# Linear attention and a squared-ReLU MLP on one Trainium2 core: the last queries of the first two batches transposed together

## The chip, the core and the metric

The kernel runs on one core of a Trainium2 chip. TensorE (PE) multiplies matrices and writes to PSUM; VectorE (DVE) and ScalarE (ACT) work element by element; SyncE (SP) issues the loads and stores; GpSimd (POOL) does almost nothing here. The metric is device time in microseconds (us), the median over runs.

## The reference

```
kv  = einsum('bhsd,bhse->bhde', k, v)            # 8 batches, 8 heads, 576 rows, 64 features
out = einsum('bhsd,bhde->bhse', q, kv)
x   = out / sqrt(mean(out * out, -1) + 1e-6) * g_norm
x   = x.transpose(0, 2, 1, 3).reshape(4608, 512)
g   = maximum(x @ w_in, 0) ** 2                  # w_in 512 x 2048
out = g @ w_out                                  # w_out 2048 x 512
```

The weights arrive as float64 and are converted to float32 on the chip.

## The kernel before

**Attention.** For each batch b and pair of heads p, `transposed_query(b, p)` brings the queries into the layout with features on the partitions, and `key_value(b, p)` forms the 64x64 products of keys and values. A batch has 576 rows: four tiles of 128, and 64 rows left over. The left-over rows of two batches make one more tile of 128; for batches 0 and 1 these are the last queries, `q_rest[0]`, loaded by two DMAs of 64 rows (L156). In batches 0 and 1 queries are transposed on PE (L339) into a PSUM tile `t_ps` and copied out by ACT (L341); with b = 1, each call also transposes two heads of `q_rest` into `tr_ps` (L345) and copies them into `qT_rest` (L348). In later batches DVE transposes. Products of keys and values gather in `kv_ps` (L357), and two ACT copies (L359, L360) take them to `kv_all`. `t_ps`, `kv_ps` and the later `xt_ps` share the tag "at" of a PSUM pool with two buffers, taken by turns. `products_x` (L388) multiplies queries by key-value products into `x_ps`; it reads `qT_rest` for the left-over rows. Then come squares on ACT (L397), sums and inverse roots on DVE (L400 to L411) and the scaled rows `x_n` (L429), which are transposed (L475) for the MLP. In the text, T(b, p) stands for the transposed query and kv(b, p) for the keys-values of that batch and pair.

**Weights.** They are loaded as 32 raw pieces, 16 of each matrix (L198), into a pool of eight buffers; each is converted by two ACT instructions (L210, L213) and four on DVE (L222 to L231). The last pieces of w_out are summed into blocks `wt` and stored to a scratch tensor in DRAM (L281), from which `w_blk` is loaded later (L662, L665).

**MLP.** The 4608 rows are taken in nine strips of 512. The first strip's up-projection runs plainly (L614), into PSUM tags A (two buffers), B and C (one each), which ACT reads with Relu and Square (L621, L622). Its down-projection and all later strips use sums of blocks so that seven products do for eight (L578, L768), with DVE forming the sums (L248, L605); in the first strip's down-projection the sums of the weight blocks (`w_t`) are also stored to DRAM (L698).

**Order.** The schedule is written out by hand: each engine takes its instructions strictly in the order in which the program issues them, and waits where an operand or a buffer is not ready. Attention work is a list `slices`; the loop over the MLP's steps calls `attend(n)` after each step, which issues slices up to index n. During the first strip, one slice of batch 1 follows each step from the sixth last up-projection step on: T, kv, T, kv, and so on. With `n` counting those steps, the eight slices of batch 1 fill n = 1 to 8; then groups of four slices (query, normalized, two of features) follow by threes. Each step also calls `convert` for weights, and starts loads on SP's queue: those of batch 1's pairs, of the left-over keys and values (L148), and of `q_rest` (L156), between steps 5 and 9.

Of the kernel before, what the change touches and what calls it, by code (L numbers as in the profile page):

```python
# [10 lines left out]
FP32 = mybir.dt.float32  # L11
# [9 lines left out]
def kernel(  # L21
# [34 lines left out]
    nc = tc.nc  # L56
    P = 128
# [4 lines left out]
    NP = H // 2  # L62
    FC = d_ff // P
    C = S // P
# [10 lines left out]
    Q_ON_PE = 2  # L75
# [17 lines left out]
    apsum = ctx.enter_context(tc.tile_pool(name="apsum", bufs=2, space=bass.MemoryType.PSUM))  # L93
# [46 lines left out]
    q_rest = {}  # L140
# [3 lines left out]
    def load_rest(b, eng):  # L144
        h = b % 2
        half = slice(REST * h, REST * (h + 1))
        for t, src in ((k_rest[half], k), (v_rest[half, h], v)):
            eng.dma_start(out=t, in_=src[b, :, C * P : S].rearrange("h s d -> s h d"))  # L148

    def load_q_rest(b, eng):  # L150
        h = b % 2
        if h == 0:
            q_rest[b // 2] = rest_pool.tile([P, H, D], FP32, name="q_rest", tag="q_rest")
        src = q[b, :, C * P : S]
        if b < Q_ON_PE:
            eng.dma_start(out=q_rest[b // 2][REST * h : REST * (h + 1)], in_=src.rearrange("h s d -> s h d"))  # L156
            return
        t = squares(q_rest[b // 2])
        for a in range(4):
            hq, f = divmod(a * SQ, D)  # L160
            for kq in range(2):
                eng.dma_start(
                    out=t[ts(a, SQ), 2 * h + kq], in_=src[hq::2, ts(kq, SQ), f : f + SQ].rearrange("p i f -> i p f")
                )
# [4 lines left out]
    def load_next(q_eng=nc.sync):  # L169
        u = next(to_load, None)  # L170
        if u is not None:
            load(*u, q_eng)
# [82 lines left out]
    def sums_in(g):  # L255

        nc.scalar.activation(w_in[:, :, g, 0:4], w_in[:, :, g, 0:4], AF.Copy, scale=g_col)
        a11, a21, a12, a22, s1, s2, s4 = (w_in[:, :, g, b] for b in range(7))
        nc.vector.tensor_tensor(out=s1, in0=a21, in1=a22, op=ALU.add)
        minus(nc.vector, s2, s1, a11)  # L260
        minus(nc.vector, s4, a12, s2)
        minus(nc.vector, a21, a11, a21)
# [24 lines left out]
    def convert(n):  # L287
        while converted[0] < min(n, len(conversions)):
            fn, a = conversions[converted[0]]
            fn(a)  # L290
            converted[0] += 1

    ident = const.tile([P, P], FP32, name="ident")
# [23 lines left out]
    qT, kvd, x_n, xt = {}, {}, {}, {}  # L317
    flat = lambda t: t.rearrange("p h d -> p (h d)")

    def open_rest(b):  # L320
        t = qt_pool.tile([P, NP, P], FP32, name="qT_rest", tag="qT_rest", bufs=1)
        for p in range(NP):
            qT["rest", b // 2, p] = t[:, p]
        return t

    def transposed_query(b, p):
        t = main.pop(("q", b, p))
        if b >= Q_ON_PE:
            qT[b, p] = qt_pool.tile([P, C, P], FP32, name="qT", tag="qT")
            nc.vector.transpose(out=flat(qT[b, p]), in_=flat(t))  # L330
            if b % 2 and p == NP - 1:
                nc.vector.transpose(
                    out=open_rest(b).rearrange("p q (k t) -> p q k t", k=4),
                    in_=squares(q_rest[b // 2]).rearrange("p k q f -> p q k f"),
                )
            return
        ps = apsum.tile([P, C, P], FP32, name="t_ps", tag="at")
        for c in range(C):
            nc.tensor.transpose(ps[:, c, :], flat(t[:, c]), ident)  # L339
        qT[b, p] = qt_pool.tile([P, C, P], FP32, name="qT", tag="qT")  # L340
        nc.scalar.copy(qT[b, p], ps)  # L341
        if b % 2:
            t = q_rest[b // 2][:, 2 * p : 2 * p + 2]
            ps = apsum.tile([P, 2, C * P], FP32, name="tr_ps", tag="x", bufs=1)[:, 0, 0:P]
            nc.tensor.transpose(ps, flat(t), ident)  # L345
            if p == 0:
                open_rest(b)
            nc.scalar.copy(qT["rest", b // 2, p], ps)  # L348

    def key_value(b, p):  # L350
        tk, tv = main.pop(("k", b, p)), main.pop(("v", b, p))
# [157 lines left out]
    slices, ready = [], {}  # L509
# [10 lines left out]
    for b in range(1, B):  # L520
        for p in range(NP):
            slices += [(transposed_query, (b, p)), (key_value, (b, p))]
        first_n = b // 2 * PAIR + (C if b % 2 else 0)
        ns = list(range(first_n, first_n + C + b % 2))
        for i in range(0, len(ns), 2):
            slices += [(query, (ns[i : i + 2],)), (normalized, (ns[i : i + 2],))]
            for n in ns[i : i + 2]:
                slices.append((features if b < X_ON_PE else squares_x, (n,)))
                if n % NT == NT - 1:
                    ready[n // NT] = len(slices)  # L530
    slice_at = [0]

    def attend(n):
        while slice_at[0] < min(n, len(slices)):
            fn, a = slices[slice_at[0]]
            fn(*a)
            slice_at[0] += 1
# [64 lines left out]
    def sums_g(s, g):  # L602
        dest = quarters(s, g)
        s1 = gq[s, 1, g] = sum_pool.tile([P, 2, TH], FP32, name="g_s1", tag="sum")
        nc.vector.tensor_tensor(out=s1, in0=dest[12], in1=dest[22], op=ALU.add)  # L605
        minus(nc.vector, dest[12], dest[11], dest[12])
# [134 lines left out]
    def leaf_sums(s, p):  # L741
        a = gq[s, A_G[p]]
        a11, a12, a21, a22 = (a[:, ts(f, FQ // 2), ts(t, P)] for t in range(2) for f in range(2))
        s1, s2, s3, s4 = (sum_pool.tile([P, FQ // 2, P], FP32, name=f"g_s{i}", tag="sum") for i in range(4))
        leaf[p] = {1: a11, 2: a12, 3: s4, 4: a22, 5: s1, 6: s2, 7: s3}
        nc.vector.tensor_tensor(out=s1, in0=a21, in1=a22, op=ALU.add)
        minus(nc.vector, s2, s1, a11)
        minus(nc.vector, s4, a12, s2)
        minus(nc.vector, s3, a11, a21)
# [85 lines left out]
    for s in range(N_STRIP):  # L835
        attend(ready[s])
        if s == 0:
            steps = [(2, up_first, (g, fh, i)) for g in range(NG) for fh in range(2) for i in range(2)]
        else:
            steps = [(1, up, (s, g, p)) for g in range(NG) for p in ORDER]  # L840
        n_up = len(steps)
        if s < DEEP:

            steps += [(2, down, (s, p, i)) for p in (ORDER if s else (1, 2, 5, 6, 7, 3, 4)) for i in range(2)]
        else:
            steps += [(2, down_deep, (s, k, i)) for k in range(7) for i in range(2)]
        goal = ready.get(s + 1, len(slices))
        total, done = sum(w for w, _, _ in steps), 0
        for i, (w, fn, a) in enumerate(steps):
            if s == 0 and i < n_up:  # L850

                convert(5 + (3 * i + 2) // 4)
                if i in (5, 7, 9):
                    load_next()
                if i == 6:
                    load_q_rest(0, nc.sync)
                    load_rest(1, nc.sync)
                    load_q_rest(1, nc.sync)
            elif s == 0 and i == n_up:
                convert(len(conversions))  # L860
                conv.close()
                sum_pool = ctx.enter_context(tc.tile_pool(name="sum", bufs=8, reuse_waits="tile"))
                stream_pool = ctx.enter_context(tc.tile_pool(name="stream", bufs=4, reuse_waits="tile"))
            if s == 0 and n_up <= i < n_up + NG:
                sums_g(0, i - n_up)
            fn(*a)
            done += w
            if s:
                attend(ready[s] + int((goal - ready[s]) * min(done / (0.42 * total), 1)))
                if s >= DEEP and i == n_up - 3:  # L870
                    leaf_sums(s, 4)
                continue
            if i == n_up + 11:
                load_next()
            if i == n_up + 13:
                load_rest(2, nc.sync)
                load_q_rest(2, nc.sync)
            if i - n_up in (7, 9, 11, 13):
                sums_in((i - n_up - 7) // 2)
            if i == n_up + 11:  # L880
                sums_x(1)
            if i == len(steps) - 1:
                stream(2)

            n = i + 1 - (n_up - 6)
            pairs, m = divmod(max(n - 2 * NP, 0), 3)
            attend(min(ready[0] + min(max(n, 0), 2 * NP) + 4 * pairs + (0, 2, 2)[m], goal))


# [28 lines left out]
```

## Time and profile before

| | |
|---|---|
| median of nine runs | 940.37 us (939.13 to 942.24) |
| the profiled execution's own time | 940.37 us |
| its span | 938.5 us |
| PE busy | 912.4 us, 97% |
| DVE busy | 685.2 us, 73% |
| ACT busy | 226.0 us, 24% |
| the four transposes of `q_rest` (L345) | 0.27 to 0.30 us each, starting between 74.2 and 101.0 us |
| their four copies (L348) | 0.27 us each |
| PE waiting for the load of `q_rest` | 3.9 us, once |
| DMA, mean over the span | 204 GB/s; 282 GB/s between 64 and 72 us |

Matmuls overlap in the pipeline, so the distance between two starts says more of their cost than the duration of one. A wait in the profile is time in which an engine stood, with the event that ended it. A granted clock below 1.00 means that PE's work took longer by that ratio.

### The profile page before, as it was taken

Reading aid. Unit: us, or ns where it says so; the run is one execution under the profiler, and the core shown is the slowest. Engines: PE = TensorE matmul, PEld = TensorE weight load, DVE = VectorE, ACT = ScalarE, POOL = GpSimd, SP = SyncE. Lnnn points to the kernel's source line nnn. Section 1 sums busy time; section 2 is a strip of 40 time slices with the busy share of each in tenths; the row PEclk is TensorE's granted clock in tenths of the full one; section 3 lists DMA queues with packets and bytes.
Section 4 is the critical chain, followed back from the end, with each engine's and each line's share of the span. In section 5 each row is a group of like instructions: output and inputs, shape, how many; then the busy total and the mean of one; then the engine's idle time right before and its main releaser. Section 6 shows DMA issues by size and latency. Waiting matters only on the chain.

```text
span 938.5 us, 17429 instructions
## 1 busy us (share of the span) xinstructions
PE 912.4 (97%) x7048; PEld 807.0 (86%) x7048; DVE 685.2 (73%) x1195; ACT 226.0 (24%) x497; POOL 1.7 (0%) x7
## 2 busy tenths in 40 slices
PE   5898999999999999999999999999999999999998
PEld 4444877889988998899889998899889988998898
DVE  4998887479846995489748974697559854983496
ACT  4796342220023102310222013201220022002200
POOL 0000000000000000000000000000000000000000
PEclk9899999999999999999999999999999999999999
DMA  9799988746964585558564875477516831682075
GB/s 280 260 285 297 310 289 294 202 112 243 303 177 99 211 291 183 128 165 320 190 145 134 297 242 138 98 292 253 173 27 246 290 99 57 235 289 71 0 262 176
DMA packets 165295, 191.46 MB, mean 204 GB/s; under 512 B 84064, under 2 KB 137824, under 8 KB 156640
## 3 DMA queue, kind: packets, MB, share of 16 engines
q1 hardware_dynamic: 164896, 190.23, 63.2%
q8 instruction: 55, 0.90, 0.4%
q14 instruction: 24, 0.20, 0.1%
q10 hardware_dynamic: 320, 0.13, 0.1%
HBM read 159.12 MB, written 31.20 MB: 203 GB/s over the span
## 4 chain that ended last, share of the span: by engine, by line
PE 87%; DVE 6%; DMA 3%; issue 1%; ACT 1%; SPq 1%; DVEq 0%; ACTq 0%
PE ps_A L578 25%; PE ps_B L768 21%; PE ps_A L768 16%; PE ps_B L578 13%; PE ps_C L578 6%; PE kv_ps L357 2%; PE x_ps L388 2%; DVE w_c L228 1%; PE ps_C L614 1%; DMA w_blk<-w_out 1%; DVE w_in L231 1%; PE ps_A L614 1%; DMA q_rest<-in_q_dram 1%; DVE w_c L222 1%; DMA raw<-in_moe_w_in_dram 1%
## 5 line engine op out<-in xcount | busy, mean ns | idle before, releaser
L578 PE MATMUL ps_A<-x_t,w_in 128*128 128x256 f32 x768 | 183.1, 381 | 0.0
L578 PEld LDWEIGHTS ps_A<-x_t,w_in 128*128 128x128 f32 x768 | 144.5, 190 | 20.1
L768 PE MATMUL ps_B<-w_blk,g_s 128*128 128x128 f32 x1024 | 124.8, 275 | 0.0
L768 PEld LDWEIGHTS ps_B<-w_blk,g_s 128*128 128x128 f32 x1024 | 119.5, 192 | 0.0
L768 PE MATMUL ps_B<-w_blk,gt 128*128 128x128 f32 x768 | 96.2, 275 | 0.0
L768 PE MATMUL ps_A<-w_blk,g_s 128*128 128x128 f32 x768 | 93.6, 275 | 0.0
L768 PEld LDWEIGHTS ps_B<-w_blk,gt 128*128 128x128 f32 x768 | 91.5, 192 | 0.4
L768 PEld LDWEIGHTS ps_A<-w_blk,g_s 128*128 128x128 f32 x768 | 89.6, 192 | 0.0
L637 DVE TENSOR_TENSOR gt<-ps_A,snap 128x512 f32<-128x512 f32 x32 | 22.1, 690 | 75.4 <-PE ps_A L578 75.4
L768 PE MATMUL ps_A<-w_blk,gt 128*128 128x128 f32 x576 | 72.2, 275 | 0.0
L638 DVE SCALAR_TENSOR_TENSOR gt<-gt 128x512 f32<-128x512 f32 x96 | 66.4, 692 | 3.3
L637 DVE TENSOR_TENSOR gt<-ps_C,snap 128x512 f32<-128x512 f32 x32 | 22.1, 690 | 63.6 <-PE ps_C L578 63.6
L768 PEld LDWEIGHTS ps_A<-w_blk,gt 128*128 128x128 f32 x576 | 68.2, 192 | 0.0
L588 ACT COPY snap<-ps_A 128x512 f32<-128x512 f32 x66 | 38.7, 586 | 117.1 <-PE ps_A L578 103.6
L578 PE MATMUL ps_A<-xT,w_in 128*128 128x256 f32 x256 | 61.3, 382 | 0.0
L578 PE MATMUL ps_C<-xT,w_in 128*128 128x256 f32 x256 | 61.1, 381 | 0.0
L578 PE MATMUL ps_B<-x_t,w_in 128*128 128x256 f32 x256 | 61.0, 381 | 0.0
L578 PE MATMUL ps_B<-xT,w_in 128*128 128x256 f32 x256 | 61.0, 381 | 0.0
L248 DVE TENSOR_TENSOR gt<-gt 128x2048 f32<-128x2048 f32 (+1 forms) x29 | 59.9, 2065 | 0.1
L782 DVE TENSOR_TENSOR o_sb<-o_sb,ps_B 128x256 f32<-128x256 f32 (+1 forms) x128 | 49.4, 386 | 12.2 <-ACT o_sb L783 4.2
L578 PEld LDWEIGHTS ps_B<-x_t,w_in 128*128 128x128 f32 x256 | 48.2, 190 | 6.7
L578 PEld LDWEIGHTS ps_B<-xT,w_in 128*128 128x128 f32 x256 | 48.2, 190 | 6.7
(118 smaller groups left out, 1106.2 us busy)
## 6 DMA issues: line engine op xcount, KB each, us to landing
w_blk<-w_deep SPq DMA_DIRECT2D x56, 1024.0 KB, 5.3
w_blk<-w_out SPq DMA_DIRECT2D x56, 768.0 KB, 4.9
raw<-in_moe_w_in_dram SPq DMA_DIRECT2D x16, 512.0 KB, 6.1
raw<-in_moe_w_out_dram SPq DMA_DIRECT2D x16, 512.0 KB, 5.3
k<-in_k_dram SPq DMA_DIRECT2D x29, 256.0 KB, 2.9
v<-in_v_dram SPq DMA_DIRECT2D x29, 256.0 KB, 3.3
w_deep<-w_t SPq DMA_DIRECT2D x7, 1024.0 KB, 5.5
x_d<-x_q SPq DMA_DIRECT2D x27, 256.0 KB, 2.1
```

Of the source, the lines that this page charges most:

```text
L222: yield nc.vector.tensor_scalar(out=c, in0=c, scalar1=LEAST, scalar2=MOST, op0=ALU.max, op1=ALU.min)
L228: yield nc.vector.scalar_tensor_tensor(out=ci, in0=high, scalar=-(2**30), in1=ci, op0=ALU.bitwise_and, op1=ALU.bitwise_or)
L248: eng.tensor_tensor(out=out, in0=a, in1=b, op=ALU.subtract)
L357: nc.tensor.matmul(ps[ts(h, D)], lhsT=a, rhs=w, start=c == 0, stop=c == C)
L388: nc.tensor.matmul(ps[half, r, i, ts(p, D)], lhsT=q[row, half], rhs=kvd[b, p][row, row], start=True, stop=True)
L578: nc.tensor.matmul(bank[BANK[p]][:, i, :], lhsT=lhsT(k), rhs=rhs(k), start=p in (1, 5, 2) and i == 0 and k == 0, stop=k == n - 1, skip_gro ...
L588: nc.scalar.copy(snap[p], b)
L614: nc.tensor.matmul(ps, lhsT=w_in[:, kc % KH, g, kc // KH * 2 + fh, ts(i, P)], rhs=xt[0][:, :, kc, :], start=kc == 0, stop=kc == NP - 1,)
L637: nc.vector.tensor_tensor(out=o, in0=b, in1=a, op=ALU.add)
L638: nc.vector.scalar_tensor_tensor(out=o, in0=o, scalar=0.0, in1=o, op0=ALU.max, op1=ALU.mult)
L768: nc.tensor.matmul(chain[c][x][:, i, :], lhsT=a[:, f, :], rhs=w[:, f, :], start=p not in (6, 7, 3) and j in ((1, 2) if place(s, p) is LAST ...
L782: add = lambda out, a, b: nc.vector.tensor_tensor(out=out, in0=a, in1=b, op=ALU.add)
```

## The change

In `transposed_query` the transposes of `q_rest` are taken out. A new slice `rest_queries(b)` transposes all four pairs of heads into one PSUM tile and takes them out with one ACT copy of 128x512. It is put in the list behind the last keys-values of batch 1, and the count in the loop is raised by one from n = 8 on, so that the slice is issued together with kv(1, 3) and all later slices stay at their steps.

```diff
         qT[b, p] = qt_pool.tile([P, C, P], FP32, name="qT", tag="qT")
         nc.scalar.copy(qT[b, p], ps)
-        if b % 2:
-            t = q_rest[b // 2][:, 2 * p : 2 * p + 2]
-            ps = apsum.tile([P, 2, C * P], FP32, name="tr_ps", tag="x", bufs=1)[:, 0, 0:P]
-            nc.tensor.transpose(ps, flat(t), ident)
-            if p == 0:
-                open_rest(b)
-            nc.scalar.copy(qT["rest", b // 2, p], ps)
+    def rest_queries(b):
+        ps = apsum.tile([P, 2, C, P], FP32, name="tr_ps", tag="x", bufs=1)[:, 0]
+        for p in range(NP):
+            nc.tensor.transpose(ps[:, p], flat(q_rest[b // 2][:, 2 * p : 2 * p + 2]), ident)
+        nc.scalar.copy(open_rest(b), ps)
...
             slices += [(transposed_query, (b, p)), (key_value, (b, p))]
+        if b % 2 and b < Q_ON_PE:
+            slices.append((rest_queries, (b,)))
...
-            attend(min(ready[0] + min(max(n, 0), 2 * NP) + 4 * pairs + (0, 2, 2)[m], goal))
+            attend(min(ready[0] + min(max(n, 0), 2 * NP) + (n >= 2 * NP) + 4 * pairs + (0, 2, 2)[m], goal))
```

On PE the first transposes of `q_rest` stood behind T(1, 0) and now all four stand behind kv(1, 3), ahead of the first half of the down-projection's second product. On ACT the four copies go and the one copy comes behind the copies of kv(1, 3). DVE, SP and POOL keep their instructions and their order.

## The prediction

> **What bounds the kernel now.** I read the page's busy shares first, then the waits of PE, then PE's timeline where its longest late wait lies, then the granted clock there, then ACT's timeline and the loads, and last the chain of waits.
>
> The shares say that PE is the bound (97%), so that only time in which PE stands still, or runs at a low clock, can be won.
>
> ```profile
> PE 912.4 (97%) x7048; PEld 807.0 (86%) x7048; DVE 685.2 (73%) x1195; ACT 226.0 (24%) x497; POOL 1.7 (0%) x7
> ```
>
> Of PE's waits (engine, line, releaser: us in total, times, longest), the first below is the one that the change touches.
>
> ```profile
> PE tr_ps L345 <- DMA q_rest<-in_q_dram: 3.9, 1, 3.9
> PE xt_ps L475 <- DVE x_n L429: 1.6, 1, 1.6
> PE ps_B L578 <- DMA w_blk<-w_out: 1.1, 1, 1.1
> ```
>
> PE's timeline (start, us, what, idle before). The reader is to see the idle time ahead of 74.19, the slow eight matmuls after it (5.36 against 3.60 for the same eight at 84.43), and the two places where the new stand is worked out: 96.30 and 109.07.
>
> ```profile
> 69.67 0.60 PE L339 MATMUL t_ps<-ident,q 128*128 128x128 f32 x4
> 74.19 0.30 PE L345 MATMUL tr_ps<-ident,q_rest 128*128 128x128 f32 x1 [3.92 <-DMA q_rest<-in_q_dram]
> 74.33 5.36 PE L614 MATMUL ps_C<-xT,w_in 128*128 128x512 f32 x8
> 79.61 0.69 PE L357 MATMUL kv_ps<-v,k 128*64 128x64 f32 x16
> ...
> 84.43 3.60 PE L614 MATMUL ps_B<-xT,w_in 128*128 128x512 f32 x8
> ...
> 96.30 0.69 PE L357 MATMUL kv_ps<-more_qkv 128*64 128x64 f32 x16
> ...
> 109.07 0.34 PE L388 MATMUL x_ps<-kv_all,qT_rest 64*64 64x64 f32 x8
> ```
>
> The clock by stretches (PE busy, PEclk, DMA share, GB/s): it falls to half one microsecond after PE has resumed.
>
> ```profile
> 74.00:75.00 1.00, 0.81 (x3) 1.00 0.77 224
> 75.00:76.00 1.00, 1.00 (x2) 0.56 1.09 358
> 76.00:77.00 1.00, 1.00 (x2) 0.50 1.03 263
> 78.00:79.00 1.00, 1.00 (x3) 0.73 1.06 244
> ```
>
> ACT's timeline a little later. ACT takes its work in order, and stands 3.52 us for the last-but-one raw piece of w_out; behind that stand the reads of ps_B and the two copies that free the buffer of kv_ps.
>
> ```profile
> 89.80 0.67 ACT L210 ACTIVATE w_c<-raw 128x512 f32<-128x512 f32 x1 [3.52 <-DMA raw<-in_moe_w_out_dram]
> 91.58 0.67 ACT L210 ACTIVATE w_c<-raw 128x512 f32<-128x512 f32 x1 [0.53 <-DMA raw<-in_moe_w_out_dram]
> 92.72 0.37 ACT L621 ACTIVATE gt<-ps_B 128x256 f32<-128x256 f32 x1
> 94.17 0.19 ACT L359 COPY kv_all<-kv_ps 64x64 f32<-64x64 f32 x1
> 94.37 0.21 ACT L360 COPY kv_all<-kv_ps 64x64 f32<-64x64 f32 x1
> ```
>
> The chain of waits runs from q_rest's load over PE to x_ps, then over DVE to a load of w_blk that PE awaits: what x_ps gains or loses goes on to the end.
>
> ```profile
> 67.05 7.00 DMA q_rest<-in_q_dram
> ...
> 109.14 1.14 PE x_ps L388 x64
> ...
> 110.30 0.60 ACT sq L397
> ...
> 110.93 1.29 DVE ms L400 x2
> ...
> 131.09 8.36 DMA w_blk<-w_out
> ```
>
> **The change part by part.** Times are those of the profiled execution: span 938.5 us, its own time 940.37 us, so 1.87 us lie around the span; 940.37 is also the median of the nine runs.
>
> *The wait goes.* PE ends T(1,0) at 70.11 (69.67 + 0.44, the distance from T(1,1) at 83.88 to the next instruction at 84.32). Up to the product at 74.33 lie 4.22 us of standing and transposing, and the half clock costs 5.36 - 3.60 = 1.76. Keys-values (1,0) then start at 70.11 + 3.53 = 73.64 (3.53: from 84.43 to kv at 87.96) instead of 79.61. Nothing new stops PE there: k_rest and v_rest of batch two land at 65.44 + 7.0 = 72.4 and 66.37 + 6.8 = 73.2. T(1,1) comes at 77.9, its queries landed by 71.7 + 4.4 = 76.1.
>
> *What is late next.* From kv(1,0) to kv(1,2) are 96.30 - 79.61 = 16.69 us, of which two transposes of 0.11 go: PE reaches kv(1,2) at 73.64 + 16.47 = 90.1, that is 6.2 us early. kv_ps and t_ps share two buffers by turns (tag "at"), so kv(1,2) needs the copies of kv(1,1) out, L359 and L360. These ended at 94.58, while PE came at 96.30: 1.7 us of slack, never visible as a wait. They are not PE's to hasten. ACT reaches them only behind L210 of the last two raw pieces; those were issued at 84.26 and 84.87 and landed 5.5 and 6.6 us later, at 89.8 and 91.5. SP issued without a pause before them, 75.22 to 85.33, under a DMA share about 1. Of that queue only one entry waits for PE, k of (1,3), which reuses the buffer of kv(1,0): issued 80.34, the entry before it done at 80.18, so at most 0.16 us earlier. I take the copies out at 94.45 (bounds 94.4 and 94.6) and PE at 94.55, with 0.1 us from release to matmul (0.14 in the chain at 74.05). The gain at kv(1,2) is 96.30 - 94.55 = 1.75, and PE has stood 4.4 us, no less than the 4.08 before.
>
> *The clock.* The row nearest to a stand of 4.4 us is that of 4.08 us: 1.76 lost. At the shortest, the stands of 1.64 and 1.09 us lost nothing (PEclk 1.00 from 139 to 143); at the longest, the low clock from 27.3 to 34.2 (PEclk 0.67 from 27 to 28, 0.92 from 34 to 35, 0.50 between), around stands of 1.11 and 2.34, lay on dense work from 29.67 on: 4.5 us at half, 2.25 lost. Bounds 0 and 2.25; I take 1.75.
>
> The Trainium skill ("TensorE: Matmul & The Clock Gate", The HAM clock gate) says that the clock falls after at least one idle window of about 3.4 us, windows which run freely. Read strictly, a stand of 4.4 us holds a whole window only in about (4.4 - 3.4) / 3.4, some 3 in 10, of the phases, and by that my sum would mostly lack the clock's part and end near 939.0. The trace disagrees: the low clock lay from 75.1 to 78.5 (0.56 and 0.73 in the rows above), 3.4 us, and in the 3.4 us before it PE had already done 0.9 us of matmuls; a window partly in use counted as idle.
>
> *The transposes and the copy.* Three of the four single transposes (0.11 each) stood before 94.55 and go into the stand. Between kv(1,2) and x_ps, one of 0.11 goes and four come, 0.44 by T's row of the same shape: +0.33 on PE. On ACT four copies of 0.27 become one of 128x512, 0.57 to 0.59 by L341's row, 0.5 less. New is that x_ps awaits the whole copy; PE has the first half of product two in between (3.65 us, 105.42 to 109.07), while ACT needs about 0.5 for kv_all and 0.59: hidden by some 2.5 us, and worth at most 1.1 if that cover went. Behind x_ps stands the second half of product two. SP's and POOL's queues keep their order, and no load is added; q_rest's buffer is reused at 161.6, far off.
>
> *Sum at x_ps:* -1.75 + 1.75 + 0.33 = +0.33 us.
>
> *Behind x_ps.* DVE takes the sums of squares at 110.93 after standing for ACT; it was free at 109.23, so x_ps could win at most 1.7 us (about 2.1 if DVE's last conversions come 0.4 earlier, raw piece 28 having landed at 80.6 and L210 begun at 81.61). From there DVE hardly stops up to 130.5 and w_blk's loads follow it, so +0.33 goes through to the end.
>
> **Forecast.** 940.37 + 0.3 = 940.7: no change, the stand moved from q_rest to kv(1,2). Within 0.2% (1.9 us) is about what a measurement of this kernel can tell from no change.
>
> **The rivals.**
>
> *The clock holds.* For: a shorter stand than I think, or a phase that suits. Against: the row at 74. It gives -1.75 + 0.33 = -1.4: 939.0, still within 0.2%.
>
> *The wait goes and does not return.* If raw pieces 30 and 31 land early enough (by some 4 us) or the copies come ahead, PE is at x_ps 5.8 us earlier; DVE then gives 1.7 to 2.1 and no more, 938.3 to 938.7. Were DVE's work to move with it, all of 6.2 - 0.33 = 5.9 would stay, 934.5. For: ACT's copies are short and PE's wait is plain. Against: DMA share about 1 up to 88 us, and ACT's 3.52 us of standing.
>
> *Slower: the raw pieces land later.* Before, 1.7 us of slack at kv(1,2) took up a late landing; afterwards each microsecond of it goes to x_ps. Raw landings in this stretch ran from 3.8 to 8.9 us. At 8.9 instead of 6.6, +2.3 + 0.33 = +2.6, 943.0; from 1.6 us later on it counts as slower. For: saturated queues. Against: nothing here adds a load or moves one.
>
> *The change does nothing at all*: excluded, since the wait named in the trace is that of the instruction moved.
>
> **How the numbers follow.** Stand moved, clock lost, 0.55, own range 939.6 to 941.8 (clock bounds 0.8 lower, 0.5 higher, 0.5 for runs); clock holds 0.10; wait gone for good 0.19, of which most lies between 938.7 and 937, little below; raw late 0.16. Faster by over 0.2%: nearly all of the third and a little of the second, 0.20. Slower: the fourth, with a little of the first, 0.18. Same 0.62. The range leaves out the far end of the third and a little of the fourth: 937.3 to 942.9.
>
> **What would show it.** PE's wait for q_rest gone, and the product behind T(1,0) eight matmuls in 3.60; a stand of about 4 us ahead of kv(1,2), released by ACT's L360; the half clock near 92 to 99 instead of 75 to 78.5; L210's waits for raw unmoved near 89.8; x_ps at 109.4. Wrong if kv(1,2) starts before 93, if no half clock follows, or if DVE's sums of squares start before 110.

## The result, and the profile after

The changed kernel takes 943.18 us, the median of 18 executions (938.8 to 946.7); the kernel before took 940.4 over all its executions beside it (937.2 to 943.5). The ratio is 1.0028, with a 95% interval of 1.0020 to 1.0037: slower by 2.8 us. The forecast was 940.7, no change, with a range of 937.3 to 942.9; the time lies above both.

The profiled execution of the changed kernel took 939.89 us (span 937.8). That is among its shortest, so it shows the mechanism but not the loss. Three more profiles of the same kernel, under the experiments, show the loss.

The busy shares, on the page after, are as before: no engine has more work.

```profile
PE 911.9 (97%) x7048; PEld 807.8 (86%) x7048; DVE 684.9 (73%) x1195; ACT 225.9 (24%) x494; POOL 1.7 (0%) x7
```

PE's waits between 60 and 165 us (engine, line, releaser: us in total, times, longest). The line for `q_rest` (3.9 us) is gone, and a line for `kv_ps`, released by ACT, has come. The two lines for `w_blk` have grown from 0.5 and 1.1. All lines of the attention code behind the edit have moved up by two: L355 and L358 are what L357 and L360 were.

```profile
PE ps_A L578 <- DMA w_blk<-w_out: 1.8, 1, 1.8
PE xt_ps L473 <- DVE x_n L427: 1.6, 1, 1.6
PE ps_B L578 <- DMA w_blk<-w_out: 1.6, 1, 1.6
PE kv_ps L355 <- ACT kv_all L358: 1.4, 1, 1.4
```

PE's timeline after (start, us, what, idle before). Behind T(1,0) the eight products now follow at once and take 3.60 us instead of 5.36. PE is ready for kv(1,2) at 92.4 and stands 1.45 us there. The four transposes stand together at 102.85, and x_ps begins at 106.89 instead of 109.07.

```profile
71.89 0.60 PE L339 MATMUL t_ps<-ident,q 128*128 128x128 f32 x4
72.32 3.60 PE L614 MATMUL ps_C<-xT,w_in 128*128 128x512 f32 x8
75.85 0.69 PE L355 MATMUL kv_ps<-v,k 128*64 128x64 f32 x16
...
93.84 0.69 PE L355 MATMUL kv_ps<-more_qkv 128*64 128x64 f32 x16 [1.45 <-ACT kv_all L358]
...
102.85 0.66 PE L345 MATMUL tr_ps<-ident,q_rest 128*128 128x128 f32 x4
103.34 3.62 PE L578 MATMUL ps_C<-w_in,gt 128*128 128x256 f32 x16
106.89 0.34 PE L386 MATMUL x_ps<-kv_all,qT_rest 64*64 64x64 f32 x8
```

The stretches just behind this stand (its length, then the busy time of PE, PEld, DVE, ACT and POOL, PEclk, DMA share, GB/s) show a full clock, as do those around 75 us: this execution lost none.

```profile
75.00:76.00 1.00, 1.00 (x7) 0.24 (x7) 1.00 (x4) 1.00 (x2) 0.00 (x0) 1.00 1.29 254
76.00:77.00 1.00, 1.00 (x21) 0.81 (x20) 1.00 (x5) 0.97 (x4) 0.00 (x0) 1.00 1.09 344
...
94.00:95.00 1.00, 1.00 (x22) 0.91 (x21) 1.00 (x3) 0.94 (x4) 0.00 (x0) 1.00 1.15 345
95.00:96.00 1.00, 1.00 (x7) 0.87 (x6) 1.00 (x5) 1.00 (x3) 0.00 (x0) 1.00 1.13 356
```

ACT's timeline after. Its stand for the last-but-one raw piece ends at 89.45, much as before (89.80), and the copy that frees `kv_ps` ends at 93.79.

```profile
89.45 0.68 ACT L210 ACTIVATE w_c<-raw 128x512 f32<-128x512 f32 x1 [4.27 <-DMA raw<-in_moe_w_out_dram]
90.80 0.68 ACT L210 ACTIVATE w_c<-raw 128x512 f32<-128x512 f32 x1
93.58 0.21 ACT L358 COPY kv_all<-kv_ps 64x64 f32<-64x64 f32 x1
```

The chain of waits no longer passes through `q_rest`; it passes through the raw piece and, as before, later through a load of w_blk.

```profile
84.74 5.97 DMA raw<-in_moe_w_out_dram
94.64 3.65 PE ps_A L578 x16
...
130.23 8.83 DMA w_blk<-w_out
139.11 7.19 PE ps_B L578 x32
```

Even in this lucky execution little stays: x_ps is 2.2 us earlier than in the profile before, but the two waits for w_blk take 3.4 us together instead of 1.6, and the next transposes of `x_n` start at 162.56 instead of 163.18, 0.6 us earlier.

### The profile page after: what moved, and what is told of

Same layout as the page of the kernel before. It is cut to its first block, busy times and chain, and to the rows that moved or that the text cites. A ratio compares the mean times of both kernels' runs of the same rounds, so it can differ in the third digit from the quotient of the medians.

```text
span 937.8 us, 17426 instructions
## 1 busy us (share of the span) xinstructions
PE 911.9 (97%) x7048; PEld 807.8 (86%) x7048; DVE 684.9 (73%) x1195; ACT 225.9 (24%) x494; POOL 1.7 (0%) x7
## 4 chain that ended last, share of the span: by engine, by line
PE 87%; DVE 6%; DMA 4%; ACT 2%; issue 1%; SPq 1%; DVEq 0%; ACTq 0%
PE ps_A L578 25%; PE ps_B L768 21%; PE ps_A L768 16%; PE ps_B L578 13%; PE ps_C L578 7%; PE kv_ps L355 2%; PE x_ps L386 2%; DVE w_c L228 1%; DMA k_rest<-in_k_dram 1%; DMA w_blk<-w_out 1%; DVE w_in L231 1%; DVE w_c L222 1%; DMA raw<-in_moe_w_in_dram 1%; DMA raw<-in_moe_w_out_dram 1%; DMA q<-in_q_dram 0%
## 5 line engine op out<-in xcount | busy, mean ns | idle before, releaser
L768 PE MATMUL ps_B<-w_blk,gt 128*128 128x128 f32 x768 | 96.2, 275 | 0.0
```

The costliest lines, as they stand in the source:

```text
L768: nc.tensor.matmul(chain[c][x][:, i, :], lhsT=a[:, f, :], rhs=w[:, f, :], start=p not in (6, 7, 3) and j in ((1, 2) if place(s, p) is LAST ...
```

## The experiments

The theory after the result: the products come to kv(1,2) about 6 us early and there meet the copies of kv(1,1), which stand on ACT's queue behind the last two raw pieces of w_out. How late these land differs from execution to execution. The kernel before has slack there; the changed one pays every microsecond, and the half clock that a long stand brings besides. The rivals: that the four transposes together, or the one wide copy, cost the time; and that the clock alone does.

### The changed kernel again

> The changed kernel once more, for another execution's profile: the one shown took 939.9 us where the median is 943.2, and its PE came 2.2 us later to T(1,0) than that of before. Theory A (clock): a usual execution has PE early, a stand of 4 us or more ahead of kv(1,2) behind ACT's copies, and then the half clock for more than one stretch of 3.4 us, so that x_ps comes 1 to 3 us later than the 109.1 of before; median 942.5 to 943.5. Theory B (loss behind x_ps): x_ps at 107 to 109.3, and 2 to 4 us more of standing after 110, at w_blk's loads. Theory C (load): the last raw pieces land 2 us or more later than 91.5, without a half clock.

Measured: 944.94 us (941.39 to 947.15) against 940.5, ratio 1.0040 (1.0024 to 1.0056). The profiled execution took longer than the first one did (span 943.9). PE's timeline shows three stands and two stretches of low clock.

```profile
74.36 0.34 PE L355 MATMUL kv_ps<-v_rest,k_rest 128*64 128x64 f32 x4 [1.16 <-DMA v_rest<-in_v_dram]
...
88.61 0.66 PE L339 MATMUL t_ps<-ident,more_qkv 128*128 128x128 f32 x4 [2.05 <-ACT qT L341]
89.10 5.29 PE L614 MATMUL ps_C<-xT,w_in 128*128 128x512 f32 x8
97.95 1.12 PE L355 MATMUL kv_ps<-more_qkv 128*64 128x64 f32 x16 [3.55 <-ACT kv_all L358]
...
99.21 5.80 PE L578 MATMUL ps_A<-w_in,gt 128*128 128x256 f32 x16
```

ACT's timeline names what the two longer ones stand for: two pairs of raw pieces, each later than in the profile before (81.61 and 89.80).

```profile
84.03 0.67 ACT L210 ACTIVATE w_c<-raw 128x512 f32<-128x512 f32 x1 [5.42 <-DMA raw<-in_moe_w_out_dram]
...
93.25 0.67 ACT L210 ACTIVATE w_c<-raw 128x512 f32<-128x512 f32 x1 [4.69 <-DMA raw<-in_moe_w_out_dram]
...
97.69 0.21 ACT L358 COPY kv_all<-kv_ps 64x64 f32<-64x64 f32 x1
```

What follows: the place and the releaser of the last stand are those of the forecast. Its end is not: 97.9 instead of 94.55. The other two stands, 1.16 us for `v_rest` and 2.05 us ahead of T(1,2), the forecast did not have. Of the expectations, A (half clock) and C (late pieces; the last landed at 94.8) showed together, and the median lies above A's 942.5 to 943.5. For B, PE's waits for w_blk are 2.9 us instead of 1.6, less than the 2 to 4 more that it asked for.

### ACT's order in the changed kernel

```diff
-        for i in range(acted[0], min(ids[-1] + 3, len(sources))):
+        for i in range(acted[0], min(ids[-1] + (3 if ids[-1] < len(sources) - 3 else 1), len(sources))):
```

ACT's conversions of the last two raw pieces now stand behind its reads of ps_B and its copies of kv(1,1).

> The changed kernel with ACT's conversions of the last two raw pieces put behind its reads of ps_B and its copies of kv(1,1), instead of ahead of them; DVE, SP and PE keep their order. ACT then frees kv_ps by about 85 us, and no stand is left ahead of kv(1,2). Theory A: stand and half clock gone, x_ps by 105 to 107, DVE's sums of squares held by DVE's own work at 108.5 to 109.5, 938 to 939.5 us. Theory B: the time stays at 942.5 to 943.5. Theory C: 939 to 941, DVE late by the late landing alone.

Measured: 941.16 us (937.43 to 943.19), ratio 1.0002 (0.9986 to 1.0017), beside the same executions of the kernel before against which the changed kernel had 1.0040. The stand at kv(1,2) is gone: the copies are out at 86.65 and kv(1,2) starts at 88.96 without a wait. So the loss is paid in ACT's queue behind the raw pieces. But x_ps at 102.67, 6.4 us earlier than in the profile before, brought no gain. PE's timeline, then DVE's, say why.

```profile
107.32 2.75 PE L578 MATMUL ps_B<-w_in,g_s 128*128 128x256 f32 x12
113.54 2.08 PE L578 MATMUL ps_B<-w_in,g_s 128*128 128x256 f32 x4 [3.47 <-DVE g_s L605]
```

```profile
103.65 0.69 DVE L605 TENSOR_TENSOR g_s<-gt 128x512 f32<-128x512 f32 x1 [2.39 <-DMA w_out<-wt]
```

The last four columns of g_s come from DVE behind its other work, and DVE itself had stood for a store of `wt`. DVE began this read at 103.95 in the profile before and at 103.59 in the first one after: PE's lead does not bring DVE forward. PE stood 3.47 us, and ran at a low clock after that (2.08 us for four products that took 1.13 at full clock elsewhere). The median lies above theory A's 938 to 939.5 and just above C's 939 to 941.

### ACT's order in the kernel before

The same edit on the kernel before.

> The kernel before with only ScalarE's conversions of the last two raw pieces put behind its reads of ps_B and its copies of kv(1,1). If the block of ScalarE by the raw pieces is hit only because the change brings the products to kv(1,2) earlier, the kernel before, which comes there at about 96 us with no wait, gains nothing: 940 to 941.3 us, ratio 0.999 to 1.001. If the pieces land late in the kernel before too and it pays for them in many executions, the edit gains as it did on the changed kernel (944.9 to 941.2, 3.8 us): 937 to 939 us, ratio 0.996 to 0.998.

Measured: 940.73 us (937.98 to 943.89), ratio 0.9999 (0.9987 to 1.0010). The edit that takes back the loss of the changed kernel does nothing here that can be measured. The raw pieces' place on ACT costs the kernel that comes to kv(1,2) early, and not the kernel before.

### The wait put back

```diff
+        if (b, p) == (1, 0):
+            ps = apsum.tile([P, 2, C * P], FP32, name="wait_ps", tag="x", bufs=1)[:, 0, 0:P]
+            nc.tensor.transpose(ps, flat(q_rest[0][:, 0:2]), ident)
```

The changed kernel, with one transpose of `q_rest` behind T(1,0) whose result nobody reads.

> The changed kernel with the wait put back: one transpose of q_rest, its result used by nothing, behind T(1,0), where the kernel before has its first one. The four transposes and the one copy stay behind kv(1,3). Theory A+C (the stand moved to kv(1,2), where the late raw pieces and a half clock are paid in full): PE again waits 4 us for q_rest, comes to kv(1,2) near 96 with ACT's copies out, 940 to 941 us, 2 to 4 faster than the changed kernel. Rival D (the four transposes together and the wide copy ahead of x_ps cost the time): 942.5 to 945, as the changed kernel.

Measured: 940.57 us (938.55 to 943.04), ratio 1.0000 (0.9989 to 1.0012). The four transposes together and the wide copy stay in this kernel and, with the wait in place, cost nothing that can be measured. Without the wait the loss is there, with it the loss is gone. PE's timeline of its profile shows the wait short, and no low clock behind it (six of the eight products in 2.80 us):

```profile
73.32 0.30 PE L344 MATMUL wait_ps<-ident,q_rest 128*128 128x128 f32 x1 [1.90 <-DMA q_rest<-in_q_dram]
73.46 2.80 PE L617 MATMUL ps_C<-xT,w_in 128*128 128x512 f32 x6
```

### The wait removed, the transposes and copies still single

The four single transposes and copies of the kernel before, moved from `transposed_query` to the end of `key_value` for the same pair:

```diff
     def transposed_query(b, p):
...
-        if b % 2:
-            t = q_rest[b // 2][:, 2 * p : 2 * p + 2]
...
     def key_value(b, p):
...
+        if b == 1:
+            t = q_rest[b // 2][:, 2 * p : 2 * p + 2]
...
```

> The kernel before with each single transpose of q_rest and its copy behind kv(1,p) instead of behind T(1,p): the wait of 4 us goes, as in the changed kernel, but there are still four transposes and four copies, one for each pair. Theory A+C: 942.5 to 945 us, a stand of 2 to 4.5 us ahead of kv(1,2). Rival D: 940 to 941.

Measured: 941.4 us (939.24 to 946.02), ratio 1.0006 (0.9991 to 1.0021). Its profile has the stand of the changed kernel, 4.66 us ahead of kv(1,2), and the low clock behind it; in the median it lost less. The interval overlaps that of the change and that of no change, so this run does not say whether the removed wait alone is worth all of the 0.28%. Neither expectation (942.5 to 945, 940 to 941) was met. With the change, 1.0020 to 1.0037, the run shares only 1.0020 to 1.0021, so that it is not excluded that part of the loss needs both, the missing wait and the four transposes together.

### Filling the stand

Products of 128x512 that nobody reads, ahead of kv(1,2) in the changed kernel, or ahead of the transpose of `q_rest` in the kernel before, keep PE busy through the stand and so take away the clock's part.

```diff
+        if (b, p) == (1, 2):   # (1, 0) in the kernel before
+            warm = apsum.tile([P, 2, C * P], FP32, name="warm_ps", tag="x", bufs=1)[:, 0]
+            for _ in range(7):   # 4 in the second pair of runs
+                nc.tensor.matmul(warm, lhsT=ident, rhs=xt[0][:, :, 0, :], start=True, stop=True)
```

> The changed kernel with seven products of 128x512 (3.0 us of PE, results used by nothing) put ahead of kv(1,2), where PE stands anyhow: the stand shrinks to about 1.4 us, and PE's clock has no reason to fall. Theory A: no half clock between 88 and 105, x_ps at 107 to 108, 938.5 to 940 us, faster than the changed kernel by 3 to 4. Theories B and C: the time stays at 942.5 to 943.5, since the end of the stand is ACT's and not PE's.

> The kernel before with seven products of 128x512 (3.0 us of PE, results used by nothing) ahead of the first transpose of q_rest, which waits 4 us for its load: the wait shrinks to about 1.1 us. Theory A: the half clock behind it goes, kv(1,2) could start at 94.5, where ACT's copies stand in the way for less than 0.5 us; x_ps at 107.3 to 107.6, 938.4 to 939.2 us. If the half clock costs nothing in the end (theory B), 940.4 as before.

Measured: 943.37 us, ratio 1.0025 (1.0012 to 1.0038), and 943.18 us, 1.0026 (1.0014 to 1.0038). Here my price of the fill was too low. Each float32 product shows as two matmuls in the trace, 0.86 us in all, and seven take 6.0 us, more than the stand. PE's timeline of the filled kernel before, where x14 counts these matmuls:

```profile
71.64 6.17 PE L345 MATMUL warm_ps<-xT,ident 128*128 128x512 f32 x14
77.87 0.33 PE L349 MATMUL tr_ps<-ident,q_rest 128*128 128x128 f32 x1
78.04 3.60 PE L618 MATMUL ps_C<-xT,w_in 128*128 128x512 f32 x8
```

So I repeated both with four products, 3.4 us.

> The fill ahead of kv(1,2) again, with four products in place of seven. One product is two passes, 0.86 us, so that the seven were 6.0 us and longer than the stand; four are 3.4 us. Theory A (the half clock behind the stand is the cost): no half clock between 85 and 105, 940.0 to 941.5 us, 2 to 3 faster than the changed kernel. Theory C alone (late pieces): 942.5 to 945, since the fill hastens no load.

> The kernel before with four products (3.4 us) in its wait for q_rest, in place of seven (6.0 us): 0.7 us of standing are left. Theory A: no half clock behind it, PE at kv(1,2) by 94.5, ACT's copies out at 94 to 96.5 in this and other executions, x_ps at 107.5 to 109, 939 to 940.5 us. If PE's lead there is worth nothing, 940.5.

Measured: 942.5 us (940.36 to 945.79), ratio 1.0015 (1.0001 to 1.0030), and 940.89 us (938.7 to 942.87), 0.9993 (0.9979 to 1.0006). By the medians the fill takes back about half of the loss in the changed kernel, and next to nothing in the kernel before. The first interval overlaps that of the change, and 942.5 lies outside the range of theory A (940 to 941.5), at the edge of that of theory C (942.5 to 945).

The granted clock of every execution gives a like division, as an estimate. Time at half clock is 2 x (1 - mean clock) x span, if every lowered clock is counted as half. Its mean is 11.9 and 12.7 us for the changed kernel (two sets of executions) and 8.5 to 9.7 for the kernel before (four sets); it fell to 7.1 and 6.8 with the four products. Some 3 us more at half clock are 1.5 us of time: by this count half of the loss is the clock's, and the other half would be that of PE's later start at kv(1,2). The division is rough: in the kernel before, the fill took away 2.3 us of half clock (9.1 to 6.8), worth 1.1 us, and the time moved by 0.0007, inside the noise.

### The last raw pieces ahead of the loads of pair (1,3)

SP issues the loads of pair (1,3) just ahead of the last two raw pieces. In these two runs the raw pieces go first.

```diff
+        if (b, p) == (1, 1):   # in transposed_query
+            load_next()
...
-            if b == 1 and p < 2:
+            if b == 1 and p == 1:
```

> The changed kernel with the loads of pair (1,3) issued behind the last two raw pieces instead of ahead of them; nothing else moves. Theory C (the stand ends when the last raw pieces have landed, and these hang on SP's queue): the pieces are issued about 4 us earlier, near 80 to 81, ACT's copies of kv(1,1) are out by 91 to 92, the stand ahead of kv(1,2) is under 2 us, and 938 to 940 us result, 3 to 5 faster than the changed kernel. If the landing does not follow the place in the queue (the transfers themselves are the limit): 942 to 944.

> The same move of loads in the kernel before. There PE comes to kv(1,2) at 96, later than ACT's copies in most executions. Theory C: 939.5 to 940.5, at most the late executions are won. If earlier conversions alone were worth time (DVE's work ahead of x_ps): 938 to 939.

Measured: 940.88 us (937.28 to 943.96), ratio 0.9985 (0.9967 to 1.0004), in the changed kernel, and 940.41 us (938.39 to 943.58), 0.9985 (0.9966 to 1.0004), in the kernel before. The kernel before without the edit had 941.47 us beside them. Issuing the pieces earlier takes the loss back too. But the changed kernel is then no better than the kernel before with the same edit, and neither is faster than the kernel before beyond doubt; the 938 to 940 expected of the first was missed. In the profile of the changed one (943.96 us, the longest of its twelve) the piece was issued at 82.50, where 80 to 81 was expected, and ACT still had it only at 91.47; the order of the issue is not the only thing that makes it late.

### Both edits together

> The change with both edits: the loads of pair (1,3) issued behind the last two raw pieces, and ScalarE's conversions of these two pieces behind its reads of ps_B and its copies of kv(1,1). If the late raw pieces and their place on ScalarE are the whole of what the change pays, nothing stands ahead of kv(1,2), the four-column reads g_s come as early as x_ps does, and the 2.5 to 3 us that the products come earlier at x_ps stay: 937.5 to 939.5 us, ratio 0.997 to 0.999. If VectorE's chain (w_out behind the stores of wt, then g_s) sets the time once the stand is gone, as one profile of the conversion-order run shows (3.47 us for g_s at 113.5), x_ps is early and the gain is lost there: 940 to 941.5 us, ratio 0.999 to 1.001.

Measured: 940.11 us (936.52 to 942.32), ratio 0.9989 (0.9975 to 1.0003). The stand at kv(1,2) is gone here too. PE's timeline of its profile shows what came in its place, and DVE's the reason of the second:

```profile
91.85 0.69 PE L357 MATMUL kv_ps<-more_qkv 128*64 128x64 f32 x16
...
97.58 0.63 PE L341 MATMUL t_ps<-ident,q 128*128 128x128 f32 x4 [1.28 <-DMA q<-in_q_dram]
...
116.12 1.13 PE L580 MATMUL ps_B<-w_in,g_s 128*128 128x256 f32 x4 [2.35 <-DVE g_s L607]
```

```profile
106.23 0.69 DVE L607 TENSOR_TENSOR g_s<-gt 128x512 f32<-128x512 f32 x1 [3.11 <-DMA w_out<-wt]
```

The loads that were moved back are now awaited (1.28 us), and DVE stands again for the stores of `wt`. The first of the two expectations (937.5 to 939.5) fell, the rival's 940 to 941.5 held. In these runs, each wait that was removed in this stretch made room for a wait for another transfer of the same crowded queue.

### The kernel before again, and four more profiles of both

No edit: the profile of another execution of the kernel before, then two of each kernel, all four on one chip.

> The kernel before once more, for a second profile of it. Theory C: ACT's copies of kv(1,1) out somewhere from 92 to 98 us here as well, without a stand ahead of kv(1,2) unless later than 96. If the change itself makes the pieces land late, 92 to 95 again.

> The changed kernel as it is, one more profile, for the landing of the last two raw pieces. If without the wait for q_rest they come later by the change itself (loads of batch two's pairs, freed earlier by the products, crowd the stores of wt and the raw loads), the copies of kv(1,1) end 25 to 29 us behind the start of T(1,0) and kv(1,2) waits for them by 2 us or more. If the late landing in one earlier profile (29.4, against 21.9 in another) was chance, it is 21 to 25 us as in the kernel before, and the stand is 1.5 us or less.

> The kernel before as it is, one more profile, for the same landing: 23 to 25 us from the start of T(1,0) to the end of the copies of kv(1,1), which kv(1,2) meets with no wait; a wait of 2 to 4 us for q_rest. If late landings happen to both kernels alike, values of 26 or more are seen here too.

> The changed kernel as it is, a second profile for the same question. Late by the change itself: 25 to 29 us from T(1,0) to the copies of kv(1,1). Late by chance: 21 to 25 us.

> The kernel before as it is, a second profile for the same question: 23 to 25 us if only the changed kernel has late landings, 26 or more in some if both have them.

The eight profiles of the two kernels, in us; "copies out" is the end of the second copy of kv(1,1), L360 or L358:

| | T(1,0) | raw piece 30 issued | copies out | kv(1,2) | stands up to kv(1,2) | x_ps | x_ps behind T(1,0) | span |
|---|---|---|---|---|---|---|---|---|
| before, first profile | 69.67 | 84.26 | 94.58 | 96.30 | 3.92 for q_rest | 109.07 | 39.4 | 938.5 |
| before, e11 | 69.02 | 81.70 | 92.0 | 92.62 | 2.58 | 105.38 | 36.4 | 935.6 |
| before, e15 | 70.75 | 84.02 | 94.58 | 94.63 | 2.66 | 107.40 | 36.7 | 937.9 |
| before, e17 | 68.73 | 83.03 | 94.47 | 95.13 | 3.54 | 107.90 | 39.2 | 937.2 |
| after, first profile | 71.89 | 83.83 | 93.79 | 93.84 | 1.45 for kv_all | 106.89 | 35.0 | 937.8 |
| after, e1 | 68.52 | 87.18 | 97.90 | 97.95 | 1.16, 2.05, 3.55 | 113.61 | 45.1 | 943.9 |
| after, e14 | 71.43 | 86.19 | 96.13 | 96.18 | 4.25 | 111.45 | 40.0 | 940.3 |
| after, e16 | 68.93 | 86.76 | 96.82 | 96.87 | 2.43, 4.59 | 111.53 | 42.6 | 940.4 |

From T(1,0) to x_ps the kernel before took 37.9 us on average, the changed one 40.7: +2.8, as much as the loss, though the four of the changed kernel alone run from 35.0 to 45.1. In e14 and e16, of the changed kernel, the copies were out 24.7 and 27.9 us behind T(1,0), and kv(1,2) waited for 4.25 and 4.59 us. In e15 and e17, of the kernel before, it was 23.8 and 25.7; neither reaches the 26 that would have shown late landings there.

Counted from T(1,0) the two kinds overlap: the 24.7 of e14 lies in the range named for a chance landing, its stand of 4.25 us in that for a late one. The issue says more: in three of four profiles of the changed kernel, raw piece 30 is issued 1.9 to 2.9 us later than in the latest profile of the kernel before. Once issued, the pieces take hardly longer: the last one landed 6.2 to 7.0 us after its issue in these three, 6.6 in the first profile before. SP's queue shows where the issue slips. The kernel before, e15:

```profile
75.14 1.07 SPq L198 DMA_DIRECT2D raw<-in_moe_w_out_dram  x2
76.79 3.50 SPq L281 DMA_DIRECT2D w_out<-wt  x4
80.39 1.73 SPq L125 DMA_DIRECT2D k<-in_k_dram  x1
...
84.02 1.08 SPq L198 DMA_DIRECT2D raw<-in_moe_w_out_dram  x2
```

and the changed kernel, e16:

```profile
76.28 1.06 SPq L198 DMA_DIRECT2D raw<-in_moe_w_out_dram  x2
77.44 5.19 SPq L281 DMA_DIRECT2D w_out<-wt  x4
82.72 2.14 SPq L125 DMA_DIRECT2D k<-in_k_dram  x1
...
86.76 1.07 SPq L198 DMA_DIRECT2D raw<-in_moe_w_out_dram  x2
```

The entries and their order are the same, and SP waits no longer for others in e16 than in e15 (2.7 against 3.4 us from the first of these lines to the last). But the four stores of `wt` hold its queue 5.19 us instead of 3.50, one of them alone 2.90, and they land 8.3 us after their issue instead of 6.0. The transfers themselves are slower. (In e14 the stores hold the queue 3.44 us only; there it is 1.6 us late at the first of these lines, and the load of k takes 2.87 us.) Between 72 and 84 us (columns as above, DMA share and GB/s last) e15, of the kernel before, and e16, of the changed one, moved:

```profile
72.00:84.00 12.00, 9.99 (x45) 4.94 (x46) 12.00 (x31) 9.99 (x25) 0.00 (x0) 1.00 1.13 317
```

```profile
72.00:84.00 12.00, 11.99 (x68) 5.71 (x67) 10.92 (x27) 6.51 (x17) 0.00 (x0) 1.00 0.94 255
```

Over the sixteen profiles of kernels with these loads in the old order, the eight with the wait for `q_rest` moved 283 to 340 GB/s in this stretch (mean 317), the eight without it 238 to 320 (mean 280); from 60 to 70 us, ahead of the change, both kinds moved about 300. Raw piece 30 was issued at 83.4 on average with the wait and at 85.4 without. The ranges overlap, and in one set of runs the difference does not show: of e1 to e4, e4 with the wait moved 283, the other three 265, 320 and 295. Why the transfers are slower without the wait, no run tells. That PE works instead of standing is hardly the whole reason: the kernel before with four products in the wait kept PE busy and moved 319, though with seven it moved 283.

## Why the prediction was wrong

*The wait goes:* right. The products behind T(1,0) follow at once at 3.60, as the step said, and kv(1,0) comes 3.53 us behind the transposes (72.32 to 75.85). "Nothing new stops PE there" was not always so: in e1 PE stood 1.16 us for `v_rest`.

*What is late next:* the place, the releaser and the two raw pieces were right, and the size was wrong. The step that failed is "I take the copies out at 94.45 (bounds 94.4 and 94.6)". These bounds came from a single profile and one argument, that the copies "are not PE's to hasten". It was true that PE could not bring them earlier. That they could come later was given to a rival, and the profiles of the changed kernel have them at 93.8, 96.1, 96.8 and 97.9, mean 96.2. The last raw piece took hardly longer from issue to landing (6.2 to 7.0 us) than the forecast's 6.6; in three of the four profiles the pieces were issued 2 to 3 us later, which "at most 0.16 us earlier" had not allowed for. The slack of 1.7 us was a long one as well: in the other three profiles of before it was 0.6, 0.05 and 0.7 us. So the gain at kv(1,2), put at 1.75, was in the mean a loss of 1.5: 96.2 against 94.7 in the four profiles of before. Two stands of 2.05 and 2.43 us ahead of T(1,2), for ACT's copy of T(1,1) behind the earlier pair of raw pieces, the forecast did not have at all.

*The clock:* "-1.75 + 1.75", the same loss on both sides, was mis-sized on both. The row that priced it, 3.92 us of waiting, was the longest of the four profiles of before; in e11 and e15 the stand was 2.6 us and cost no clock at all. The changed kernel lost none at 1.45 us, but 2.61, 2.22 and 1.61 us behind its longer stands (from kv(1,2) to T(1,3) 6.90, 6.51 and 5.90 us, against 4.29 at full clock). I had compared the longest stand of before with the stand of after. All executions together give 1.5 us more loss, by the count above. Two slips in the working: the own range of 939.6 to 941.8 takes 0.8 us for the lower bound of the clock, where the bounds stated, 0 and 2.25 around 1.75, make it 1.75, and even 0.8, 0.5 and 0.5 add up to 939.4 to 941.7; and the rows from 139 to 143 reach only the stand of 1.09 us, not that of 1.64 at 161.5, whose clock was full too.

*The transposes and the copy,* +0.33 on PE and nothing on ACT: right. From kv(1,2) to x_ps PE takes 13.05 us in the first profile after and 12.77 before, +0.28. The run with the wait put back contains them and measures 1.0000, so they are below what can be told. The copy's cover was 3.55 us in the profile after (103.34 to 106.89), no wait appeared.

*The sum at x_ps,* +0.33, was in the mean of four profiles each +3.4 (110.9 against 107.4): +1.5 at kv(1,2), +1.6 for the clock behind it and +0.3 for the transposes. Of this, 0.6 us is that PE came to T(1,0) later in the profiles after.

*Behind x_ps:* a delay goes through to the end, as the step said (e1: x_ps 4.5 us later than in the first profile of before, span 5.4 us longer). That a lead of x_ps is worth at most about 2.1 us, since DVE is not free sooner, was right too: DVE's sums of squares began 2.1 us earlier both in the profile after (108.79, x_ps 2.2 us earlier) and in e3 (108.85, x_ps 6.4 us earlier). But even these 2.1 us did not reach the end: 0.6 were left at 162.56, and e3 has a span of 938.2. Where DVE is early as well, a gain does last: in e11, of the kernel before, the pieces were issued 2.6 us earlier, x_ps came 3.7 us earlier, and the span was 2.9 us shorter.

*The rivals.* "Slower: the raw pieces land later", worked out as 943.0, came nearest to what happened, at 943.2. The pieces did land later, but not for the price it named, 8.9 us from issue to landing instead of 6.6, and by the count above half of the loss is the clock's; that the numbers agree so closely is luck. Its chance of 0.16 was too small: it was held back by "nothing here adds a load or moves one". No load was added, but in three of four profiles the stores and loads ahead of the pieces went slower. "The wait goes and does not return" gave 938.3 to 938.7 with the copies ahead. That run was made (e3) and came out at 941.2: the price had DVE's limit at x_ps, and overlooked DVE's reads for g_s, which stand behind the stores of `wt`.

Of the signs named, the wait's end and the place of the stand showed right; "L210's waits for raw unmoved near 89.8" (89.45, 90.95, 92.50 and 93.25) and "x_ps at 109.4" (106.89 to 113.61) did not. Of the three signs of being wrong, the first profile after showed two, no half clock and DVE's sums before 110 (108.79); in the other three profiles the half clock followed.

## What to carry to other kernels

A wait that is removed on the bounding engine moves to the next thing which that engine needs, and slack that one profile shows there is a sample, not a bound: take the spread of the load that sets it from several profiles, and let the range follow its late end. Before taking out a stand of 4 us, follow each of the next two or three transfers in the same queue; here the last raw pieces, the stores of `wt` and the loads of w_blk were each waited for, in one run or another, once an earlier wait was gone. 

## What the runs showed of the hardware that was not expected

**The length of a stand and the clock.** At the two places studied, ahead of the first transpose of `q_rest` and ahead of kv(1,2), the seven stands of 3.41 us or more (3.41, 3.54, 3.55, 3.92, 4.25, 4.59, 4.66) were each followed by half clock; the eight from 0.89 to 3.22 us (0.89, 1.45, 1.76, 1.90, 2.15, 2.58, 2.66, 3.22) never were. The Trainium skill ("TensorE: Matmul & The Clock Gate", The HAM clock gate) has the clock fall after at least one idle window of about 3.4 us that runs freely. By that, an estimate, a whole window fits into a stand of 3.5 us in only (3.5 - 3.4) / 3.4, some 3 in 100, of the phases, and most such stands would escape; here none did. In e14 the granted clock (length, PE busy, PEclk, DMA share, GB/s) fell while PE still stood:

```profile
93.00:94.00 1.00, 0.00 (x0) 1.00 1.15 345
94.00:95.00 1.00, 0.00 (x0) 0.53 1.15 346
```

That is some 2.1 us after PE had stopped, at 91.93. In these profiles the low clock lasts 3.4 us or twice that (75.1 to 78.5 before, 94.1 to 100.9 in e14), and in the last 3.4 us before this fall PE had worked for 1.3. The length isn't a clean bound, though: ahead of T(1,2) stands of 2.05 us (e1) and 1.92 us (e7) were followed by half clock (5.29 and 5.30 us for eight products), and one of 2.43 us (e16) was not.

**The rate of the same transfers.** With the same entries in the same order on SP's queue, the mean rate between 72 and 84 us ran from 238 to 340 GB/s, and the time at which ACT took raw piece 30 from 87.2 to 94.1 us. That the rate was lower without the wait is a difference between the means of eight profiles each; its cause stays open, and so does how much of the loss a kernel with the wait removed and the transposes left single would show (1.0006, 0.9991 to 1.0021).
